# Other PSUM banks and slots for the first query blocks, and the exact squares of 26 chunk slots on ScalarE

## The chip, the cores and the metric

The kernel runs on one core of one Trainium2 chip. The core has five engines with queues of their own: TensorE (PE in the profile, its weight loads PEld), VectorE (DVE), ScalarE (ACT), GpSimd (POOL) and SyncE (SP), which here only issues DMAs. Each engine takes its instructions strictly in the order in which the program lists them, and waits where the next one waits. The metric is the device time of one execution in microseconds, the median of several executions.

## The reference

Three stages follow each other. All arithmetic is 32-bit.

```
attention: 4 batches, 8 heads, 576 positions, head size 64, each position sees itself and the 63 before it
  scores = q k^T / 8, masked; attn = exp(scores - max) / (sum + 1e-9); x = attn v        -> x: 2304 x 512
dense:     h = max(x w_in, 0)          w_in 512 x 2048
           x2 = (h * h) w_out          w_out 2048 x 512                                 -> x2: 2304 x 512
experts:   logits = x2 w_gate (8 experts); the largest logit chooses one expert per token
           out[token] = p(expert) * (max(x2 w1[e], 0) w2[e])     w1 512 x 1024, w2 1024 x 512
```

## The kernel before, in words

**Stages.** Tokens go through attention and the dense layer in 9 stages `st` of 256 tokens. A stage has four query blocks `g` of 64 positions, so blocks 0 to 7 belong to stages 0 and 1. The dense layer of a stage is 16 chunks `f` of 128 of the 2048 hidden units. One pair (st, f) is a chunk slot. `order` lists them: five slots of stage 0, then stages 0 and 1 in turn up to slot 26, the rest of stage 1 up to slot 31, then stage after stage. The experts follow from about 500 us on.

**Three matmuls for one.** An fp32 value is split into a rounded part `h` and a remainder `l`, and `mm3` (L172 to L174) multiplies h by h, h by l and l by h. Someone has to make these pairs: for x (`halves`, L168 on ACT and L169 on DVE), for the weights, and for the squared hidden units.

**One chunk slot.** `gemm1` makes 12 matmuls into one of two PSUM banks tagged `h`, in its first 256 columns. `hidden` (L462, ACT) writes r = relu. One slot later `square` (L469, ACT) writes gh = r squared, rounded, into SBUF, and DVE (L471) writes the exact square into columns 256 to 511 of the same bank; `square_low` (L478, DVE) subtracts: gl = exact minus gh. Two slots later `gemm2` makes 6 matmuls with gh and gl into the banks `y`. The bank `h` of a slot is free for the slot after the next when L478 has read it.

**Weights of the dense layer.** They arrive as 64-bit numbers that are rebuilt as fp32, per chunk f: two DMAs of 512 KB into one of two staging buffers `stg` (L236, L234), `conv_a` on ACT (L189), `conv_b` of four DVE instructions over 1024 columns (L205, L206, L207, L210), which at its end issues the loads of chunk f+2 into the same staging buffer, and `conv_c`: two casts on ACT (L226) and two subtractions on POOL or DVE (L228). Chunks are rebuilt while slots 0 to 26 run: one per slot for the first five slots, one per two slots after that. The same `tmp` buffers, two, hold what is being rebuilt.

**One query block.** `ATT` is a chain of steps, put at slot numbers by `chain`: scores on PE (L355 adds the mask for blocks below 8, L360), maximum on DVE (L375 and L378, or L383 and L387), four exps on ACT with their row sums `tot` (L396 for blocks below 8, L403 after that), `att_norm` (L410 and L411 on DVE: tot plus 1e-9, reciprocal; L412 on POOL: the product), four transposes on PE (L418), a copy on ACT (L423), 16 matmuls with v (L433), and the split of x (L168, L169). Scores of blocks 0 to 7 lie in the banks `y` 0 and 1 in turn, so block g+2 needs the exps of block g to be over.

**Order.** Slot i runs from -8 on; slots below 0 hold attention and weight rebuilding alone. What stands at one slot is emitted there in a fixed order, and a list scheduler then orders the instructions of each engine; the order is fixed in the program.

Of the kernel before, what the change touches and what calls it, by code (L numbers as in the profile page):

```python
# [16 lines left out]
ACTF = mybir.ActivationFunctionType  # L17
ALU = mybir.AluOpType
# [31 lines left out]
def kernel(  # L50
# [13 lines left out]
    nc = tc.nc  # L64
# [6 lines left out]
    NF = DFF // P  # L71
    ST = 256
    NS = NT // ST
    TT = ST // P
    QB = ST // W
# [47 lines left out]
    for half in range(2):  # L123
# [5 lines left out]
            out=mid, in_=mid, pattern=[[-1, P]], compare_op=ALU.is_ge, fill=NEG, base=W, channel_multiplier=1  # L129
# [25 lines left out]
    def psum(tag, bufs):  # L155
        return pr.tile([P, 512], F32, tag, bufs)

    ybanks = [pspool.tile([P, 512], F32, tag=f"y{i}", name=f"y{i}") for i in range(2 * TT)]
# [24 lines left out]
    def conv_a(f):  # L183
        i = (br.at["tmp"] + 1) % 4
        assert i % 2 == 0
        c = [br.tile([P, 512], I32, "tmp", 4) for _ in range(2)]
        whole = tmp2[i // 2].rearrange("p t n -> p (t n)")
        w = stg2[f % 2].bitcast(I32).rearrange("p t (n two) -> p (t n) two", two=2)
        nc.scalar.activation(whole.bitcast(F32), w[:, :, 1].bitcast(F32), ACTF.Abs)  # L189
        conv[f] = w[:, :, 0], w[:, :, 1], whole, c  # L190
# [109 lines left out]
    def load_q(g, n=1):  # L300
        b, i = divmod(g, NB)
        if g >= NE:
            qd[g] = br.tile([P, W, HP], F32, "qd", 1)
            nc.sync.dma_start(qd[g], qT[b, :, i])
            return
        qt = qfirst[:, g:g + n]
        for j in range(n):
            qk[g + j] = qfirst[:, g + j]
        if g > 1:
            for part in (qt[:D, :, W:], qt[D:, :, :W]):  # L310
                nc.scalar.copy(part, zero[:part.shape[0]].unsqueeze(2).unsqueeze(3).to_broadcast(part.shape))
        else:
            with tc.issue_after(made.ins):
                nc.vector.memset(qt[:D, :, W:], 0.0)
                nc.vector.memset(qt[D:, :, :W], 0.0)
        for half in range(2):
            rows = slice(half * D, half * D + D)
            nc.sync.dma_start(qt[rows, :, half * W:half * W + W, :], qT[b, rows, i:i + n])

    def lay_q(g):  # L320

        qk[g] = er.tile([P, HP, 2, W], F32, "q", 2)
        if g < NE + 2:
            with tc.issue_after(made.ins):
                nc.gpsimd.memset(qk[g][:D, :, 1, :], 0.0)
                nc.gpsimd.memset(qk[g][D:, :, 0, :], 0.0)
        d = qd.pop(g).rearrange("p s h -> p h s")
        for half in range(2):
            rows = slice(half * D, half * D + D)

            if g < NE + 5:
                nc.scalar.copy(qk[g][rows, :, half, :], d[rows])
            else:
                nc.gpsimd.tensor_copy(qk[g][rows, :, half, :], d[rows])  # L334
# [4 lines left out]
    def load_k(g, n=1):  # L339
        b, i = divmod(g, NB)  # L340
        nc.sync.dma_start(kfirst[:, g:g + n] if g < NB else kring[:, g % 4:g % 4 + n], kT[b, :, i:i + n])
# [7 lines left out]
    def att_scores(g):  # L349
        qt = qk.pop(g)  # L350
        k0 = g - 1 if g % NB else g
        if g < NE:
            ps = ybanks[g % 2]
            m = mask_b[:, 0 if g % NB else 1, :].unsqueeze(1).to_broadcast([P, HP, P])
            nc.tensor.matmul(ps.rearrange("p (h k) -> p h k", h=HP), lhsT=ident_b, rhs=m, start=True, stop=False)  # L355
        else:
            ps = psum("a", 2)
        for hp in range(HP):
            kt = kfirst[:, k0:k0 + 2] if g < NB else kring[:, k0 % 4:k0 % 4 + 2] if k0 % 4 < 3 else kring[:, 3::-3]
            nc.tensor.matmul(  # L360
                ps[:, hp * P:(hp + 1) * P], lhsT=qt[:, :, hp] if g < NE else qt[:, hp], rhs=kt[:, :, hp, :], start=g >= NE, stop=g >= NE or hp == HP - 1
            )
        if NE <= g < NS * QB - 1:
            lay_q(g + 1)
        if NE <= g < NS * QB - 2:
            load_q(g + 2)
        if NB < g < NS * QB - 3:
            load_k(g + 3)
        probs[g] = ps
# [20 lines left out]
    def att_exp(g):  # L390
        s, nmax = probs[g]
        tot = br.tile([P, HP], F32, "tot", 3)
        if g < NE:
            ps, s = s, sfirst[g % 4]
            for hp in range(HP):
                nc.scalar.activation(  # L396
                    s[:, hp, :], ps[:, hp * P:(hp + 1) * P], ACTF.Exp, bias=nmax[:, hp:hp + 1], scale=SCALE,
                    accum_out=tot[:, hp:hp + 1],
                )
            probs[g] = s, tot  # L400
            return
        for hp in range(HP):
            nc.scalar.activation(  # L403
                s[:, hp, :], s[:, hp, :], ACTF.Exp, bias=nmax[:, hp:hp + 1], accum_out=tot[:, hp:hp + 1]
            )
        probs[g] = s, tot

    def att_norm(g):
        s, tot = probs[g]
        nc.vector.tensor_scalar_add(tot, tot, 1.0e-9)  # L410
        nc.vector.reciprocal(tot, tot)  # L411
        nc.gpsimd.tensor_tensor(s, s, tot.unsqueeze(2).to_broadcast([P, HP, P]), op=ALU.mult)  # L412

# [51 lines left out]
    def square(st, f):  # L465
        ps, r = gT[st, f]
        gh = br.tile([P, ST], F32R, "gh", 3)
        gl = br.tile([P, ST], F32R, "gl", 3)
        nc.scalar.square(gh, r)  # L469

        nc.vector.scalar_tensor_tensor(  # L471
            out=ps[:, ST:2 * ST], in0=ps[:, :ST], scalar=0.0, in1=r, op0=ALU.max, op1=ALU.mult
        )
        gT[st, f] = ps, gh, gl

    def square_low(st, f):
# [403 lines left out]
    slot = {c: i for i, c in enumerate(order)}  # L880
    todo = {}
    ON_PE = (att_scores, att_transpose, att_values, gate_rank, early_pick, early_rows, early_tokens)

    def at(i, f, *args):
        todo.setdefault((i, f in ON_PE), []).append((f, args))

    def run(i, pe):
        for f, args in todo.pop((i, pe), ()):
            f(*args)
# [3 lines left out]
    def chain(i, stages, x, gaps, most=2):  # L893

        for f, gap in zip(stages, gaps):
            i += gap
            if f in ON_PE and i >= 0:
                while load.get(i, 0) >= most:
                    i += 1
                load[i] = load.get(i, 0) + 1  # L900
            at(i, f, x)
        return i

    ATT = (att_scores, att_max, att_exp, att_norm, att_transpose, att_evac, att_values, att_out)
    at(16, load_gates, 0)

# [2 lines left out]
            at(i + part, gate_dots, st, part)  # L909
        chain(i + E // 2, (gate_top, gate_rank, gate_slot), st, (0, 1, 1))  # L910

    PRE = 8
    for f in range(NF):
        i = max(-3, min(f - 1, slot[0, f] - 2))
        at(i, conv_c, f)
# [5 lines left out]
                  (0, load_k, 11), (0, load_k, 12), (0, load_wg, 0), (1, lay_q, NE), (1, load_q, NE + 1)):  # L921
        at(i, *l)
    for g in range(2 * QB):
        chain(g - PRE, ATT, g, (0, 1, 0, 1, 0, 1, 0, 1))
    for g in range(2 * QB, NS * QB):
        st, j = divmod(g, QB)
        i = slot[st, 0] - 19 + 4 * j
# [17 lines left out]
    conv_a(0)  # L945
    for i in range(-PRE, len(order) + LA):
        run(i, False)
        if 0 <= i - 1 < len(order):
            square(*order[i - 1])
            square_low(*order[i - 1])  # L950
        if 0 <= i < len(order):
            gemm1(*order[i])
        if i >= LA:
            st, f = order[i - LA]
            gemm2(st, f)
            if f == NF - 1:
                x2_out(st)
        run(i, True)
        if 0 <= i < len(order):
            hidden(*order[i])  # L960
# [194 lines left out]
```

## Time and profile before

| what | value |
| --- | --- |
| median of 3 runs | 835.53 us (834.1 to 836.63) |
| profiled execution, its own time | 832.06 us |
| span of its trace | 829.9 us |
| mean granted TensorE clock | 0.987 |
| busy: PE, PEld | 95%, 83% of the span |
| busy: DVE, ACT, POOL | 64%, 48%, 33% |

The span runs from the first to the last instruction; 2.16 us of the profiled execution lie around it. Busy shares are over the whole span and mix stages. The span has three stretches: the opening, in which attention of the first blocks and the weights of the dense layer are prepared; the dense stages from about 130 us; the experts from about 500 us. A matmul's row overlaps the next one's, so a row's own time is longer than the step from one to the next; the same holds, by a few hundredths of a microsecond, for DVE and ACT.

### The profile page before, as it was taken

How to read it: one execution, taken by the hardware profiler on the slowest of the kernel's cores; microseconds unless marked ns; L12 is line 12 of the kernel's file. 1: busy time of each engine (PE TensorE's matmuls, PEld its weight loads, DVE VectorE, ACT ScalarE, POOL GpSimd, SP SyncE). 2: the span in 40 equal slices, each digit the busy share in tenths (PEclk: the TensorE clock that was granted, in tenths of full speed). 3: DMA queues.
4: the chain of work that ended last, by engine and by line, in shares of the span. 5: the costliest groups of instructions: out<-in, count | busy, mean ns of one | idle time of the engine just before them, and what ended most of it. 6: DMA issues, size and time to landing. Idle time of an engine off the chain costs nothing.

```text
span 829.9 us, 14957 instructions
## 1 busy us (share of the span) xinstructions
PE 787.3 (95%) x5212; PEld 685.5 (83%) x5212; DVE 530.4 (64%) x1198; ACT 398.8 (48%) x1051; POOL 269.9 (33%) x262
## 2 busy tenths in 40 slices
PE   6889989999999999999999999989999999999894
PEld 5777878888888888888888897877898888888783
DVE  5799995984855947639467396568678654434110
ACT  6986663434444443534344345447577553434211
POOL 4646751112121221312211016165567541420201
PEclk9989999999999999999999999999999999999998
DMA  9845553111111111102020037366678644420101
GB/s 264 274 134 190 194 172 102 64 34 32 58 45 64 39 42 62 52 29 75 26 64 18 22 102 229 104 216 208 193 244 246 212 155 131 135 80 2 51 2 43
DMA packets 50860, 91.50 MB, mean 110 GB/s; under 512 B 8220, under 2 KB 24604, under 8 KB 50752
## 3 DMA queue, kind: packets, MB, share of 16 engines
q1 hardware_dynamic: 44688, 80.43, 30.3%
q0 software_dynamic: 6064, 9.63, 3.5%
q8 instruction: 69, 1.13, 0.6%
q14 instruction: 39, 0.32, 0.1%
HBM read 84.59 MB, written 13.81 MB: 119 GB/s over the span
## 4 chain that ended last, share of the span: by engine, by line
PE 66%; issue 13%; DVE 9%; DMA 5%; ACT 4%; POOL 1%; ACTq 0%; SPq 0%; POOLq 0%; DVEq 0%
PE h L172 11%; PE h L173 10%; PE h L174 10%; PE y L172 10%; PE y L174 9%; PE y L173 9%; PE a L360 2%; DMA stg<-in_moe_w_out 2%; PE a L433 2%; PE a L418 1%; DVE tmp L205 1%; DVE tmp L210 1%; PE a L683 1%; DVE tmp L207 1%; DMA out<-s,tab 1%
## 5 line engine op out<-in xcount | busy, mean ns | idle before, releaser
L172 PE MATMUL h<-xh,w 128*128 128x256 f32 (+3 forms) x864 | 262.9, 304 | 10.9 <-DVE gl L478 5.4
L174 PE MATMUL h<-xh,w 128*128 128x256 f32 (+3 forms) x864 | 255.6, 296 | 1.2 <-POOL w L228 1.2
L173 PE MATMUL h<-xl,w 128*128 128x256 f32 (+3 forms) x864 | 255.6, 296 | 0.9 <-DVE xl L169 0.5
L172 PEld LDWEIGHTS h<-xh,w 128*128 128x128 f32 x864 | 164.9, 191 | 27.6 <-DVE gl L478 9.6
L173 PEld LDWEIGHTS h<-xl,w 128*128 128x128 f32 x864 | 165.0, 191 | 9.1 <-DVE xl L169 0.9
L174 PEld LDWEIGHTS h<-xh,w 128*128 128x128 f32 x864 | 165.0, 191 | 4.3 <-POOL w L228 1.5
L462 ACT ACTIVATE r<-h 128x256 f32<-128x256 f32 x144 | 55.1, 382 | 203.7 <-PE h L174 197.9
L172 PE MATMUL y<-w,gh 128*128 128x512 f32 x294 | 119.2, 405 | 0.7 <-ACT gh L469 0.7
L770 DVE SCALAR_TENSOR_TENSOR ggl<-h,ggh 128x512 fp32r<-128x512 f32 (+1 forms) x69 | 46.2, 670 | 111.6 <-ACT ggh L769 111.5
L173 PE MATMUL y<-w,gh 128*128 128x512 f32 x294 | 116.4, 396 | 0.0
L471 DVE SCALAR_TENSOR_TENSOR h<-h,r 128x256 f32<-128x256 f32 x144 | 61.4, 426 | 84.0 <-ACT r L462 84.0
L174 PE MATMUL y<-w,gl 128*128 128x512 f32 x294 | 102.1, 395 | 0.5 <-DVE gl L770 0.5
L769 ACT ACTIVATE ggh<-h 128x512 fp32r<-128x512 f32 (+1 forms) x69 | 40.2, 583 | 125.5 <-PE h L174 96.2
L548 DVE SCALAR_TENSOR_TENSOR tmp<-tmp,stg 128x512 f32<-128x512 f32 x128 | 96.0, 750 | 0.8
L334 POOL COPY q<-qd 64x256 f32<-64x256 f32 x46 | 34.4, 749 | 143.9 <-PE a L360 142.5
L172 PE MATMUL y<-w,ggh 128*128 128x512 f32 x170 | 70.7, 416 | 0.0
L174 PE MATMUL y<-w,ggl 128*128 128x512 f32 x170 | 67.6, 398 | 1.7 <-DVE junk L996 1.1
L173 PE MATMUL y<-w,ggh 128*128 128x512 f32 x170 | 67.1, 395 | 0.0
L276 POOL TENSOR_TENSOR w<-stg,w 128x512 fp32r<-128x512 f32 x27 | 36.5, 1357 | 90.6 <-ACT w L275 87.6
L478 DVE TENSOR_TENSOR gl<-h,gh 128x256 fp32r<-128x256 f32 x144 | 60.5, 420 | 8.3 <-ACT gh L469 1.5
L172 PEld LDWEIGHTS y<-w,gh 128*128 128x128 f32 x294 | 55.6, 189 | 10.8 <-ACT gh L469 1.4
L173 PEld LDWEIGHTS y<-w,gh 128*128 128x128 f32 x294 | 55.6, 189 | 9.4
(165 smaller groups left out, 1262.4 us busy)
## 6 DMA issues: line engine op xcount, KB each, us to landing
stg<-in_moe_w SPq DMA_DIRECT2D x45, 512.0 KB, 4.0
stgx<-in_moe_w SPq DMA_DIRECT2D x18, 512.0 KB, 4.2
stg<-in_moe_w_in SPq DMA_DIRECT2D x16, 512.0 KB, 4.0
stg<-in_moe_w_out SPq DMA_DIRECT2D x16, 512.0 KB, 4.9
v<-in_v SPq DMA_DIRECT2D x28, 256.0 KB, 2.7
x_d<-tmp SPq DMA_DIRECT2D x18, 256.0 KB, 2.0
q<-in_moe_w SPq DMA_DIRECT2D x9, 512.0 KB, 4.5
qd<-in_q SPq DMA_DIRECT2D x28, 128.0 KB, 2.1
```

What stands on the lines that cost most here:

```text
L172: nc.tensor.matmul(o, lhsT=ah, rhs=bh, start=first, stop=False)
L173: nc.tensor.matmul(o, lhsT=ah, rhs=bl, start=False, stop=False)
L174: nc.tensor.matmul(o, lhsT=al, rhs=bh, start=False, stop=last)
L276: rest.tensor_tensor(l[:, a:a + 512], src, h[:, a:a + 512].bitcast(F32), op=ALU.subtract)
L334: nc.gpsimd.tensor_copy(qk[g][rows, :, half, :], d[rows])
L360: nc.tensor.matmul(ps[:, hp * P:(hp + 1) * P], lhsT=qt[:, :, hp] if g < NE else qt[:, hp], rhs=kt[:, :, hp, :], start=g >= NE, stop=g >= N ...
L462: nc.scalar.activation(r, gT[st, f][:, :ST], ACTF.Relu)
L471: nc.vector.scalar_tensor_tensor(out=ps[:, ST:2 * ST], in0=ps[:, :ST], scalar=0.0, in1=r, op0=ALU.max, op1=ALU.mult)
L478: nc.vector.tensor_tensor(gl, ps[:, ST:2 * ST], gh.bitcast(F32), op=ALU.subtract)
L548: nc.vector.scalar_tensor_tensor(out=junk, in0=x2sb[tt], scalar=1.0, in1=w, op0=ALU.mult, op1=ALU.mult, accum_out=l[:, t, e:e + 1])
L769: nc.scalar.activation(h[:, :width], hid[f][:, :width], ACTF.Relu)
L770: nc.vector.scalar_tensor_tensor(out=l[:, :width], in0=hid[f][:, :width], scalar=0.0, in1=h[:, :width].bitcast(F32), op0=ALU.max, op1=ALU. ...
```

## The change

Three edits, and what the scheduler makes of them.

- **Banks and slots of the first blocks.** Blocks 2 and 3 get their scores in the two banks `h`, which no slot uses yet; blocks 0 and 1 keep `y` 0 and 1, and 4 to 7 go on in those in turn. The first slot number goes from -8 to -6. Blocks 0 and 1 start at -6, 2 and 3 at -5, 4 and 5 at -3 (before: -8, -7, -6, -5, -4, -3), 6 and 7 at -2 and -1 as before.
- **The 1e-9 on ACT.** For all 36 blocks it is added by an ACT instruction behind the exps instead of a DVE instruction before the reciprocal.
- **The exact squares of slots 0 to 25.** There ACT writes r squared into columns 256 to 511 of the bank `h`, and a second ACT instruction copies it, rounded, from there into gh. DVE's L471 is gone in these slots. From slot 26 on nothing changes here.

```
 def att_scores(g):
-            ps = ybanks[g % 2]
+            ps = psum("h", 2) if g in (2, 3) else ybanks[g % 2]
 def att_exp(g):                      # once in each of the two branches
+            nc.scalar.activation(tot, tot, ACTF.Copy, bias=1.0e-9)
 def att_norm(g):
-        nc.vector.tensor_scalar_add(tot, tot, 1.0e-9)
         nc.vector.reciprocal(tot, tot)
 def square(st, f):
-        nc.scalar.square(gh, r)
-        nc.vector.scalar_tensor_tensor(
-            out=ps[:, ST:2 * ST], in0=ps[:, :ST], scalar=0.0, in1=r, op0=ALU.max, op1=ALU.mult
-        )
+        if slot[st, f] < 2 * NF - 6:
+            nc.scalar.square(ps[:, ST:2 * ST], r)
+            nc.scalar.copy(gh, ps[:, ST:2 * ST])
+        else:
+            nc.scalar.square(gh, r)
+            nc.vector.scalar_tensor_tensor(
+                out=ps[:, ST:2 * ST], in0=ps[:, :ST], scalar=0.0, in1=r, op0=ALU.max, op1=ALU.mult
+            )
...
-    PRE = 8
+    PRE = 6
...
     for g in range(2 * QB):
-        chain(g - PRE, ATT, g, (0, 1, 0, 1, 0, 1, 0, 1))
+        chain(g // 2 - PRE if g < QB else max(-3, g - 2 * QB), ATT, g, (0, 1, 0, 1, 0, 1, 0, 1))
```

The line numbers of the new kernel are higher by one to eight: L396 is L397, L423 is L425, L462 is L464, L478 is L485; the new instructions are L401, L408, L474 and L475.

On ACT, in the start of the program, the kernel before has this (nmax and sf are the maxima and the exps of one block; sf_143 is block 3, tmp_76 and tmp_77 the weights of chunks 0 and 1).

```order
L396 ACTIVATE sf_140,tot_183<-y_131,nmax_178 128x128 x4
L378 ACTIVATE nmax_179<-nmax_179 128x4
L396 ACTIVATE sf_141,tot_184<-y_132,nmax_179 128x128 x4
L378 ACTIVATE nmax_180<-nmax_180 128x4
L396 ACTIVATE sf_142,tot_185<-y_131,nmax_180 128x128 x4
L189 ACTIVATE tmp_77<-stg_79 128x1024
L226 CAST w_271<-tmp_76 128x4x128
L226 CAST w_272<-tmp_76 128x512
L378 ACTIVATE nmax_178<-nmax_178 128x4
L423 COPY sf_140<-a_204 128x512
L423 COPY sf_141<-a_205 128x512
L396 ACTIVATE sf_143,tot_183<-y_132,nmax_178 128x128 x4
```

And now, in the same place:

```order
L397 ACTIVATE sf_140,tot_188<-y_131,nmax_183 128x128 x4
L379 ACTIVATE nmax_184<-nmax_184 128x4
L401 ACTIVATE tot_188<-tot_188 128x4
L397 ACTIVATE sf_141,tot_189<-y_132,nmax_184 128x128 x4
L379 ACTIVATE nmax_185<-nmax_185 128x4
L401 ACTIVATE tot_189<-tot_189 128x4
L397 ACTIVATE sf_142,tot_190<-h_203,nmax_185 128x128 x4
L379 ACTIVATE nmax_183<-nmax_183 128x4
L401 ACTIVATE tot_190<-tot_190 128x4
L189 ACTIVATE tmp_77<-stg_79 128x1024
L397 ACTIVATE sf_143,tot_188<-h_204,nmax_183 128x128 x4
```

The exps of block 3 stand ahead of the two casts of chunk 0 and the two copies of blocks 0 and 1, which followed block 2 before; blocks 2 and 3 are read from the banks h.

On ACT in the middle of the opening, around slots 8 to 10, before:

```order
L462 ACTIVATE r_461<-h_435 128x256
L469 ACTIVATE gh_81<-r_461 128x256
L462 ACTIVATE r_460<-h_434 128x256
L226 CAST w_271<-tmp_77 128x4x128
L226 CAST w_272<-tmp_77 128x512
L469 ACTIVATE gh_82<-r_460 128x256
```

And now:

```order
L464 ACTIVATE r_456<-h_204 128x256
L408 ACTIVATE tot_188<-tot_188 128x4
L332 COPY q<-qd_405 64x4x64 x2
L474 ACTIVATE h_204<-r_456 128x256
L168 CAST xh<-a_233 128x4x64
L189 ACTIVATE tmp_77<-stg_79 128x1024
L475 CAST gh_82<-h_204 128x256
L226 CAST w_243<-tmp_76 128x4x128
L226 CAST w_244<-tmp_76 128x512
```

Between relu and gh there is now one more instruction of the slot, and others can stand on either side of it.

On DVE in the same stretch, before (L205 to L210 are the weights, L471 and L478 a chunk slot):

```order
L207 SCALAR_TENSOR_TENSOR tmp_76<-stg_78,tmp_76 128x1024
L387 TENSOR_REDUCE nmax_180<-s_1063 128x4
L478 TENSOR_TENSOR gl_85<-h_434,gh_82 128x256
L210 SCALAR_TENSOR_TENSOR tmp_76<-stg_78,tmp_76 128x1024
L471 SCALAR_TENSOR_TENSOR h_435<-h_435,r_461 128x256
L478 TENSOR_TENSOR gl_83<-h_435,gh_80 128x256
L410 TENSOR_SCALAR tot_185<-tot_185 128x4
L411 RECIPROCAL tot_185<-tot_185 128x4
L205 TENSOR_SCALAR tmp_77<-tmp_77 128x1024
```

And now:

```order
L207 SCALAR_TENSOR_TENSOR tmp_77<-stg_79,tmp_77 128x1024
L485 TENSOR_TENSOR gl_83<-h_203,gh_80 128x256
L169 TENSOR_TENSOR xl<-y_133,xh 128x4x64
L210 SCALAR_TENSOR_TENSOR tmp_77<-stg_79,tmp_77 128x1024
L485 TENSOR_TENSOR gl_84<-h_204,gh_81 128x256
L205 TENSOR_SCALAR tmp_76<-tmp_76 128x1024
```

The square and the addition are gone from between the weights; the subtraction stays. The order of the DMAs on SP changes by a few places only.

## Rows read from the trace of the kernel before

**Rows 1.** The page: busy tenths of three engines in 40 slices of 20.75 us.

```profile
PE   6889989999999999999999999989999999999894
DVE  5799995984855947639467396568678654434110
ACT  6986663434444443534344345447577553434211
```

**Rows 2.** Windows: stretch, its length, busy us (count) per engine, clock, DMA share, GB/s.

```profile
10.00:70.00 60.00, 50.64 (x402) 43.70 (x402) 52.47 (x87) 52.19 (x162) 33.01 (x23) 0.94 0.70 226
34.00:70.00 36.00, 31.44 (x244) 26.47 (x245) 33.95 (x55) 31.18 (x82) 19.99 (x13) 0.91 0.48 158
54.50:61.50 7.00, 5.75 (x23) 5.13 (x24) 6.83 (x13) 6.96 (x25) 4.08 (x3) 0.51 0.34 116
70.00:130.00 60.00, 55.09 (x382) 46.62 (x381) 59.58 (x87) 36.20 (x87) 32.77 (x23) 1.00 0.54 181
130.00:480.00 350.00, 350.00 (x2578) 310.47 (x2577) 226.96 (x698) 146.38 (x475) 66.96 (x78) 1.00 0.15 46
```

**Rows 3.** Waits of PE from 70 to 130 us: us in total, times, longest.

```profile
PE h L172 <- DVE gl L478: 3.4, 6, 1.1
```

**Rows 4.** Timeline of the start: start us, us, engine, line, operation, idle before and releaser.

```profile
10.91 0.20 ACT L378 ACTIVATE nmax<-nmax 128x4 f32<-128x4 f32 x1
12.52 0.21 ACT L378 ACTIVATE nmax<-nmax 128x4 f32<-128x4 f32 x1
12.70 0.58 PE L355 MATMUL y<-mask_b,ident_b 128*128 128x512 bf16 x1 [3.25 <-ACT sf L396]
15.87 0.21 ACT L378 ACTIVATE nmax<-nmax 128x4 f32<-128x4 f32 x1 [1.59 <-DVE nmax L375]
...
17.49 1.13 ACT L189 ACTIVATE tmp<-stg 128x1024 f32<-128x1024 f32 x1
...
21.97 0.24 ACT L378 ACTIVATE nmax<-nmax 128x4 f32<-128x4 f32 x1
...
34.28 0.50 PE L172 MATMUL h<-xh,w 128*128 128x256 f32 x2 [1.11 <-ACT xh L168]
```

**Rows 5.** Groups by line, 70 to 130 us: count, busy us, mean ns, idle before.

```profile
L210 DVE SCALAR_TENSOR_TENSOR tmp<-stg,tmp 128x1024 int32<-128x1024 int32 x9 | 11.4, 1263 | 0.0
...
L471 DVE SCALAR_TENSOR_TENSOR h<-h,r 128x256 f32<-128x256 f32 x17 | 7.1, 419 | 0.0
L478 DVE TENSOR_TENSOR gl<-h,gh 128x256 fp32r<-128x256 f32 x16 | 6.6, 410 | 0.1
...
L410 DVE TENSOR_SCALAR tot<-tot 128x4 f32<-128x4 f32 x3 | 0.5, 157 | 0.0
...
L469 ACT ACTIVATE gh<-r 128x256 fp32r<-128x256 f32 x16 | 6.7, 417 | 0.4
L462 ACT ACTIVATE r<-h 128x256 f32<-128x256 f32 x17 | 6.4, 376 | 8.3 <-PE h L174 8.3
```

**Rows 6.** Timeline of DVE, 116 to 125 us: one chunk of weights and its neighbours.

```profile
116.68 1.21 DVE L210 SCALAR_TENSOR_TENSOR tmp<-stg,tmp 128x1024 int32<-128x1024 int32 x1
...
118.15 0.68 DVE L205 TENSOR_SCALAR tmp<-tmp 128x1024 f32<-128x1024 f32 x1
...
122.68 0.42 DVE L471 SCALAR_TENSOR_TENSOR h<-h,r 128x256 f32<-128x256 f32 x1
123.01 1.21 DVE L210 SCALAR_TENSOR_TENSOR tmp<-stg,tmp 128x1024 int32<-128x1024 int32 x1
...
124.48 0.68 DVE L205 TENSOR_SCALAR tmp<-tmp 128x1024 f32<-128x1024 f32 x1
```

**Rows 7.** Timelines of SP and ACT, 117 to 125 us: the staging buffer's next load.

```profile
117.96 0.38 SPq L236 DMA_DIRECT2D stg<-in_moe_w_in  x1
118.44 0.44 SPq L234 DMA_DIRECT2D stg<-in_moe_w_out  x1
...
123.21 1.20 ACT L189 ACTIVATE tmp<-stg 128x1024 f32<-128x1024 f32 x1 [2.38 <-DMA stg<-in_moe_w_out]
```

More of the change, by code (lines that the diff above doesn't have):

```diff
@@ L405, in att_exp @@
             )
+        nc.scalar.activation(tot, tot, ACTF.Copy, bias=1.0e-9)
         probs[g] = s, tot
```

## The prediction

> **What bounds the kernel now.** I read the slices of the page first [rows 1]. PE is at 9 tenths nearly everywhere; its holes before the experts lie in the first six slices, and there DVE is at 9 tenths from the third to the sixth. So I asked for windows [rows 2]. From 130 to 480 us PE is busy 350 of 350 us: nothing that the change does to DVE or ACT there can shorten anything, and what the opening gains or loses is passed on as it is. From 70 to 130 us DVE is busy 59.58 of 60 us and PE 55.09: DVE is the bound, PE idles 4.91 us. The waits of PE in that stretch say how the bound reaches it [rows 3]: six times, 3.4 us in all, the first matmul of a slot waits for L478, the subtraction that frees its bank h. From 10 to 70 us no engine is full for long: PE idles 9.4 us, DVE 7.5, ACT 7.8, and 4.56 us of PE's are behind 34 us. From 54.5 to 61.5 us, after waits of PE, the granted clock is 0.51, so nearly all of it at the lower level of 1.2 GHz: half of 7 us, some 3.4 us, is lost there.
>
> So the change can act in two places: the start, up to the first matmul of slot 0 at 34.28 us [rows 4], and the stretch to about 130 us.
>
> **The start.** Slot 0 needs blocks 0 to 3. Before, the mask of block 2 waits 3.25 us until ACT has read block 0's bank; ACT then waits 1.59 us for block 2's maximum [rows 4], and block 3's exps stand behind L189, two casts and two copies, ending at 21.97 us, where the next L378 starts. Now blocks 2 and 3 need no bank of another block. ACT's step from one block to the next is 12.52 - 10.91 = 1.61 us. Four of them, three additions of 0.21 us (the nearest row is L378 over the same 4 elements) and L189 with 1.13 us give 10.91 + 6.44 + 0.63 + 1.13 = 19.1 us for the end of block 3's exps, 2.9 us sooner. That rests on queries and keys of blocks 2 and 3 having landed by about 12.5 us; block 2's mask at 12.70 was held by ACT and its scores followed with no DMA wait. Bounds: 0, if something behind (the reciprocal behind chunk 1's weights on DVE, POOL, a landing) keeps slot 0 where it is, and 4.8 us, both waits in full. I take 3.0, since the row of ACT's step is the chain's own.
>
> Is it kept to 70 us? ACT is the engine that could take it back. By 70 us it gains 8 additions, 1.7 us, and a second instruction for seven slots, 0.42 us each, 2.9 us. Its idle time is 7.8 us [rows 2], so 3.2 us of room remain: enough for the 3.0, and for nothing more. I therefore count the other holes of PE between 34 and 70 us, and the low clock, as unchanged.
>
> **The squares.** Slots 0 to 25 lose L471 on DVE. Its row is 419 ns long [rows 5], but instructions overlap: L471 at 122.68 is followed by L210 at 123.01 [rows 6], so a square costs DVE 0.33 us. From 70 to 130 us there are 17 of them and three L410 of 0.157 us or less: 17 x 0.33 + 3 x 0.1 = 5.9 us off DVE's 59.6. Before 70 us the same saving (6 squares) lies beside an ACT that has no room, and the three after 130 us beside a full PE; both count as nothing. If that cover were gone they would be worth 9 x 0.33 = 3 us more.
>
> ACT pays: gh took one instruction (L469, 417 ns), now a square and a copy. The trace shows no ACT write from SBUF into PSUM. The nearest rows are L469 with 417 ns (SBUF to SBUF) and L462 with 376 ns (PSUM to SBUF); the price is bounded by nothing, if only the copy matters for the chain, and by 2 x 417 ns in series. I take 0.42 us per slot, by L469: 17 x 0.42 = 7.1 us more in a stretch in which ACT is busy 36.2 of 60 us. 43.3 of about 53 us is still no bound.
>
> The Trainium skill speaks against this move: "ScalarE: Activation LUTs", section "Rules for kernel authors", says to do relu, max and products on VectorE, which it gives as up to three times as fast per element in bf16. The trace does not bear that out for these fp32 tiles: L471 on DVE 419 ns, L469 on ACT 417 ns over the same 128x256 [rows 5]. By the rule ACT's part would be dear, which is the slower rival below; by the rows the two engines cost the same and only their load decides.
>
> What is late next, once DVE has room? Two things. PE itself: it idles 4.91 us there, so no more can come of it. And the staging loop: L210 at 116.68 ends at 117.89, the next load is issued at 117.96 and 118.44, L189 starts on its landing at 123.21 after a wait of 2.38 us, and L205 starts at 124.48 [rows 6, 7]. That is 6.6 us from the end of one chunk's L210 to the L205 of the chunk after the next, in which DVE had no time over. With c for DVE's time from L205 to L210 of a chunk, two chunks can't take less than 6.6 + c. Before, c is 123.01 + 1.21 - 118.15 = 6.1 us [rows 6], so the floor is 6.35 us per chunk; without two squares c is 5.4 and the floor 6.0. DVE alone would need 6.7 - 0.7 = 6.0 us, 6.7 being 60 us over the nine L210 of the stretch [rows 5]. The loop thus costs little, but it is close. Of the cap of 4.91 us I take 4.0; bounds 0 and 4.9.
>
> **The 1e-9.** On DVE it is counted. On ACT it stands behind the exps, 0.21 us later for the reciprocal; past 130 us it lies beside 350 us of full PE, with ACT busy 146 of them. Nothing, at most 36 x 0.21 us if every block stood on the path, which rows 2 exclude.
>
> **The sum.** 3.0 + 4.0 = 7.0 us off the profiled execution: 832.06 - 7.0 = 825.1 us, span 822.9 us plus 2.16 around it. The median of the runs shown is 3.5 us above that execution, and the metric is such a median: 835.5 - 7.0 = 828.5 us.
>
> **The rivals.** *Little of it.* By 70 us ACT takes the start back: the additions and copies also stand in front of the casts of the weights, which PE waits for. After 70 us the staging loop, a little longer than in rows 7, holds the chunks at their old pace. For it: L189 already waits for its DMA 2.38 us, and ACT is nearly full from 54.5 to 61.5 us, 6.96 of 7 [rows 2]. Against it: DVE's work truly shrinks by a tenth where it is the bound. It would leave 0.5 of the start and 1.0 of the rest: 834.0 us.
>
> *All of it.* The start brings 3.0, PE's idle 4.9 us after 70 us go, the low clock from 54.5 us does not come because PE no longer waits ahead of it (3.4), and 2 of the 4.56 us go too: 13.3 us, 822 us. For it: each of these is idle time of PE that hangs on DVE or ACT. Against it: ACT's room of 3.2 us, and the weights of the first five slots, which come no sooner than their DMAs.
>
> *Slower: the chain of gl through ACT.* Before, the exact square on DVE and gh on ACT ran beside each other; now relu, square, copy and subtraction follow each other, and on ACT other work (L189, casts of 1.1 us a pair, q copies) stands between square and copy. PE waits for just this, through the bank h [rows 3]. Each slot loses 0.33 us of DVE's queue ahead of gl and gains at least 0.42 us on ACT; it decides from the point where what stands between the two ACT instructions exceeds what DVE lost, some 0.3 us per slot on average. With 0.42 us more at each of 17 slots PE waits 7.1 us longer, less the 3.0 of the start: 4.1 us slower, 839.6 us. For it: six of these waits are there now. Against it: gl and the bank are each wanted only two slots after the slot's own gemm1, and DVE's queue ahead of L478 shrinks.
>
> That the change doesn't do what it says is not a rival: the rows of the instructions show both moves.
>
> **How the numbers follow.** The forecast 0.48, all of it 0.18, little of it 0.16, slower 0.18. The likeliest one's own range follows from its bounds (start 0 to 4.8, squares 0 to 4.9): both upper ends give 825.8 us, and with one lower end and the other term as taken it is 831.5 or 832.5, so 826 to 832.5 us. To hold 8 in 10 the range must take in most of "all" and "little" and the near part of "slower": 821 to 838 us. A measurement of this kernel can tell about 0.3%, 2.5 us, from no change. "Little" at 1.5 us lies within that, with a quarter of it beyond on the faster side: faster 0.48 + 0.18 + 0.04 = 0.70, same 0.12, slower 0.18.
>
> **What would show it.** In the profile after, the first matmul of slot 0 starts near 31 us instead of 34.28; if it starts at 34, the start failed. The exps of block 3 end near 19 us. From 70 to 120 us DVE is below 59.6 of 60, ACT above 43 of 60 in proportion, and L478's line as what PE waits for shrinks from 3.4 us; if it grows, the slower rival is right. L189's waits for the staging DMAs grow a little; if they grow to a microsecond per chunk and DVE idles before L205, the loop holds. The dense stages are full on PE and start some 7 us sooner. The prediction is wrong if they start at the same time or later, or over 12 us sooner.

## The result, and the profile after

The changed kernel takes 839.3 us (median of 17 runs, 835.48 to 841.76) against 834.1 us (17 runs, 831.67 to 837.11). The ratio is 1.0056, interval 1.0042 to 1.0071: 4.7 us slower, where 7.0 us faster was forecast. Its profiled execution has a span of 837.1 us (before 829.9).

Two rows of the page answer to [rows 1]:

```profile
PE   6789889999999999999999999979999999999894
DVE  5699993894764946639467387567677654434110
```

The tenths hardly move: PE's row is a tenth lower in three slices, and DVE is still at 9 from the third to the sixth. So the windows, in the columns of [rows 2], of the kernel after:

```profile
34.00:70.00 36.00, 29.25 (x236) 24.85 (x237) 34.40 (x47) 31.99 (x90) 17.86 (x12) 0.95 0.47 156
54.50:61.50 7.00, 6.68 (x46) 5.63 (x45) 6.96 (x9) 5.44 (x11) 3.12 (x3) 1.00 0.49 165
70.00:130.00 60.00, 52.40 (x372) 43.26 (x372) 58.87 (x66) 41.11 (x106) 35.61 (x25) 1.00 0.56 183
130.00:480.00 350.00, 350.00 (x2579) 310.59 (x2578) 218.55 (x670) 149.91 (x501) 67.27 (x78) 1.00 0.15 46
```

PE idles 6.75 us instead of 4.56 from 34 to 70 us and 7.60 instead of 4.91 from 70 to 130: 4.9 us more. That is about the size of the loss, but no exact account of it: by the granted clock from 34 to 70 us, 0.95 instead of 0.91, some 1.4 us of it came back (an estimate from these rows), and PE has not done the same steps by 34 us. From 130 us on PE is full as before; the last relu of the dense stages starts at 526.25 us instead of 521.41, 4.8 us later. The other 2.4 us between the two spans lie in the experts; what follows the last relu takes 308.5 us before, and 308.5 to 314.3 in the traces of the kernels of the table below. DVE has 21 instructions less from 70 to 130 us and is busy 0.7 us less.

The start, in the columns of [rows 4], the last exp of block 3 and the first two matmuls of slot 0:

```profile
18.68 0.37 ACT L397 ACTIVATE sf<-h,nmax 128x128 f32<-128x128 f32 x1
...
32.94 0.48 PE L172 MATMUL h<-xh,w 128*128 128x256 f32 x2
```

The exps of block 3 end at 19.05 us, as worked out (19.1). Slot 0 begins 1.3 us sooner, not 3.0. Groups of the kernel after, 70 to 130 us (columns of [rows 5]):

```profile
L207 DVE SCALAR_TENSOR_TENSOR tmp<-stg,tmp 128x1024 int32<-128x1024 int32 x9 | 17.0, 1891 | 0.2
L206 DVE TENSOR_SCALAR tmp<-tmp 128x1024 int32<-128x1024 int32 x9 | 12.5, 1388 | 0.1
...
L485 DVE TENSOR_TENSOR gl<-h,gh 128x256 fp32r<-128x256 f32 x15 | 6.1, 409 | 0.0
L474 ACT ACTIVATE h<-r 128x256 f32<-128x256 f32 x15 | 5.8, 387 | 0.3
L475 ACT CAST gh<-h 128x256 fp32r<-128x256 f32 x15 | 5.5, 370 | 0.2
```

The same two weight instructions in the kernel before, same stretch:

```profile
L207 DVE SCALAR_TENSOR_TENSOR tmp<-stg,tmp 128x1024 int32<-128x1024 int32 x9 | 13.8, 1530 | 0.0
...
L206 DVE TENSOR_SCALAR tmp<-tmp 128x1024 int32<-128x1024 int32 x9 | 10.2, 1137 | 0.0
```

Nothing was done to L206 and L207, yet nine of each take 5.5 us more. The squares that left took 17 x 0.33 = 5.6 us; that the two numbers nearly match is no rule, since with the order held the same squares gone lengthen the weights by 1.7 us of 7.9 (the table over 13 chunks further down).

Which waits hold PE from 34 to 130 us (us in total, times, longest)? After:

```profile
PE h L172 <- DVE gl L485: 4.3, 5, 1.7
PE a L361 <- ACT sf L425: 2.2, 1, 2.2
PE y L172 <- ACT gh L475: 1.8, 2, 1.1
PE a L435 <- DVE s L384: 1.6, 1, 1.6
PE a L361 <- DVE xl L169: 1.5, 1, 1.5
PE a L420 <- POOL s L414: 1.4, 1, 1.4
PE h L173 <- DVE xl L169: 1.0, 1, 1.0
PE a L420 <- POOL sf L414: 0.9, 1, 0.9
PE a L361 <- DVE s L384: 0.3, 1, 0.3
```

And before:

```profile
PE h L172 <- DVE gl L478: 3.7, 7, 1.1
PE a L418 <- DVE s L383: 1.5, 1, 1.5
PE h L174 <- POOL w L228: 1.2, 1, 1.2
PE h L172 <- ACT w L226: 1.1, 1, 1.1
PE h L172 <- ACT xh L168: 1.1, 1, 1.1
PE h L173 <- DVE xl L169: 0.5, 1, 0.5
PE a L360 <- DVE s L383: 0.5, 1, 0.5
PE y L172 <- ACT gh L469: 0.5, 1, 0.5
```

Read them in two heaps. The waits of chunk slots (`h` and `y`) are 8.1 us before and 7.1 after. The waits of attention steps (`a`: scores, transposes, values of a block) are 2.0 before and 7.9 after. PE takes its row strictly in order, so an attention step whose input isn't ready stops the chunk slots behind it. One such place, PE and ACT of the kernel after, 41 to 47 us:

```profile
43.30 1.16 PE L361 MATMUL a<-kf,q 128*128 128x128 f32 x8 [2.17 <-ACT sf L425]
...
46.18 0.36 PE L172 MATMUL h<-xh,w 128*128 128x256 f32 x1
```

```profile
41.05 1.31 ACT L332 COPY q<-qd 64x256 f32<-64x256 f32 x2
42.39 0.37 ACT L168 CAST xh<-y 128x256 fp32r<-128x256 f32 x1
42.66 0.59 ACT L425 COPY sf<-a 128x512 f32<-128x512 f32 x1
43.13 0.39 ACT L475 CAST gh<-h 128x256 fp32r<-128x256 f32 x1
```

The scores of block 8 stand in PE's row ahead of slot 2 and wait 2.17 us for the copy that empties their bank, which stands on ACT behind two q copies; a gh (L475) stands there too. Slot 2's first matmul starts at 46.18 us. Before, it starts at 42.16, and the scores of block 8 come behind it, at 46.39.

This place shows the mechanism, not the lag that stays. Attention steps that now stand ahead of slot 2 stood behind it before, and the next slots are level again: slot 3's relu starts at 54.76 us against 54.73, slot 6's at 68.53 against 69.06. The lag that stays comes behind 70 us. Slot 12's relu starts 2.4 us later (93.63 against 91.23), slot 24's 5.1; before, and after:

```profile
132.76 0.38 ACT L462 ACTIVATE r<-h 128x256 f32<-128x256 f32 x1 [0.63 <-PE h L174]
```

```profile
137.86 0.39 ACT L464 ACTIVATE r<-h 128x256 f32<-128x256 f32 x1 [1.59 <-PE h L174]
```

PE's waits from 70 to 130 us alone, after:

```profile
PE h L172 <- DVE gl L485: 3.8, 4, 1.7
PE a L435 <- DVE s L384: 1.6, 1, 1.6
PE a L361 <- DVE xl L169: 1.5, 1, 1.5
PE y L172 <- ACT gh L475: 0.7, 1, 0.7
```

Before, they were 3.4 us for gl [rows 3] and the 1.5 us of L418 above. So attention steps make 1.6 us of the 2.7 us more, the slots' gh and gl the rest. PE also does the transposes and values of one block more there (16 and 64 matmuls against 12 and 48), some 1.3 us by its rows (0.66 us for four transposes, 0.69 for 16 matmuls with v). What makes up the rest of this lag isn't shown.

### The profile page after: what moved, and what is told of

The parts are those of the page before. It is cut to its first block, busy times and chain, and to the rows that moved or that the text cites. A ratio compares the mean times of both kernels' runs of the same rounds, so it can differ in the third digit from the quotient of the medians.

```text
span 837.1 us, 14934 instructions
## 1 busy us (share of the span) xinstructions
PE 788.3 (94%) x5212; PEld 685.8 (82%) x5212; DVE 519.4 (62%) x1136; ACT 409.9 (49%) x1113; POOL 270.6 (32%) x262
## 5 line engine op out<-in xcount | busy, mean ns | idle before, releaser
L464 ACT ACTIVATE r<-h 128x256 f32<-128x256 f32 x144 | 55.2, 384 | 192.9 <-PE h L174 190.5
L478 DVE SCALAR_TENSOR_TENSOR h<-h,r 128x256 f32<-128x256 f32 x118 | 50.7, 429 | 79.4 <-ACT r L464 79.2
L555 DVE SCALAR_TENSOR_TENSOR tmp<-tmp,stg 128x512 f32<-128x512 f32 x128 | 94.1, 735 | 0.8
L485 DVE TENSOR_TENSOR gl<-h,gh 128x256 fp32r<-128x256 f32 x144 | 60.4, 420 | 32.0 <-ACT gh L477 15.2
L414 POOL TENSOR_TENSOR s<-s,tot 128x512 f32<-128x512 f32 x28 | 32.5, 1162 | 102.9 <-DVE tot L413 86.0
L172 PEld LDWEIGHTS y<-w,gh 128*128 128x128 f32 x294 | 55.6, 189 | 12.4 <-ACT gh L475 2.8
```

The source lines that it names most:

```text
L172: nc.tensor.matmul(o, lhsT=ah, rhs=bh, start=first, stop=False)
L464: nc.scalar.activation(r, gT[st, f][:, :ST], ACTF.Relu)
L478: nc.vector.scalar_tensor_tensor(out=ps[:, ST:2 * ST], in0=ps[:, :ST], scalar=0.0, in1=r, op0=ALU.max, op1=ALU.mult)
L485: nc.vector.tensor_tensor(gl, ps[:, ST:2 * ST], gh.bitcast(F32), op=ALU.subtract)
L555: nc.vector.scalar_tensor_tensor(out=junk, in0=x2sb[tt], scalar=1.0, in1=w, op0=ALU.mult, op1=ALU.mult, accum_out=l[:, t, e:e + 1])
```

## The experiments

All are medians over five rounds beside the kernel before on the same chip; two further runs, named below, are one execution each. Theory A: what DVE saves comes back as longer instructions beside POOL. B: the chain of gl through ACT. C: the order that the scheduler makes. D: the staging loop.

| run | median, us | ratio to before, interval | PE idle 34 to 160 us |
| --- | --- | --- | --- |
| before | 834.1 | | 9.5 |
| the changed kernel | 839.3 | 1.0056, 1.0042 to 1.0071 | 14.4 |
| squares alone | 835.9 | 1.0016, 1.0003 to 1.0029 | 11.2 |
| banks alone | 843.21 | 1.0104, 1.0076 to 1.0133 | 14.6 |
| 1e-9 alone | 839.84 | 1.0075, 1.0055 to 1.0095 | 14.8 |
| changed, L228 on DVE | 832.72 | 0.9982, 0.9966 to 0.9999 | 8.6 |
| 1e-9, old order | 833.8 | 0.9996, 0.998 to 1.0013 | 9.5 |
| squares, old order | 833.04 | 0.9988, 0.9974 to 1.0002 | 9.9 |
| banks, old order | 834.87 | 1.0011, 0.9996 to 1.0025 | 9.8 |
| all three, old order | 834.41 | 1.0005, 0.9989 to 1.0022 | 9.3 |
| before, L228 on DVE | 837.97 | 1.0041, 1.0024 to 1.0058 | 15.0 |
| all three in that order | 840.41 | 1.0079, 1.0054 to 1.0104 | 15.3 |
| squares twice, old order | 840.3 | 1.0066, 1.0043 to 1.009 | 15.6 |
| before in the order of "1e-9 alone" | 843.65 | 1.0107, 1.0082 to 1.0133 | 17.9 |
| all three, only DVE's row old | 837.41 | 1.0038, 1.0022 to 1.0055 | 11.8 |
| changed, L228 on DVE, two ACT rules | 834.04 | 1.0003, 0.999 to 1.0015 | 9.9 |
| squares, L228 on DVE | 832.54 | 0.9976, 0.996 to 0.9992 | 8.6 |
| squares, 1e-9, L228 on DVE | 836.79 | 1.0023, 1.0006 to 1.0041 | 11.7 |

The last column (126 us less PE's busy time in the window 34 to 160 us) is of the one profiled execution. It goes with the time, though not in proportion: wherever a kernel is 3 us or more slower, PE idles 2 us or more longer there. The windows behind four of its values, in the columns of [rows 2]; before:

```profile
34.00:160.00 126.00, 116.53 (x817) 100.11 (x818) 113.54 (x195) 79.39 (x202) 57.92 (x40) 0.97 0.44 146
```

the changed kernel:

```profile
34.00:160.00 126.00, 111.65 (x802) 95.32 (x803) 106.97 (x148) 86.89 (x234) 58.63 (x41) 0.99 0.45 146
```

all three edits in the old order:

```profile
34.00:160.00 126.00, 116.73 (x819) 100.85 (x820) 107.64 (x161) 89.95 (x239) 57.76 (x40) 0.97 0.45 148
```

and the kernel before in the order of "1e-9 alone":

```profile
34.00:160.00 126.00, 108.13 (x771) 91.89 (x772) 109.51 (x170) 76.50 (x201) 56.39 (x40) 0.97 0.45 148
```

The third has DVE 5.9 us less busy than the first, and PE as busy: DVE's relief did not reach PE. Of PE's waits from 34 to 160 us in the third, those for gl are down from 3.7 us and those for gh, now behind a square and a copy on ACT, up from 0.5; its waits for xh and xl, for weights from ACT and POOL and for s stay, 5.3 us of them against 5.9:

```profile
PE y L172 <- ACT gh L473: 2.6, 3, 2.1
PE h L172 <- DVE gl L483: 1.9, 4, 1.0
```

In the fourth DVE and PE are both less busy than in the first: PE waits for gl and gh (further down), and DVE is idle 16.5 us instead of 12.5.

**One edit at a time.** The first edit alone is `psum("h", 2) if g in (2, 3)` with PRE and chain, the second the 36 additions, the third the `if slot[st, f] < 2 * NF - 6` of `square`. The fourth run is the changed kernel with

```
-            low = nc.vector if (2 * f + which) % 6 == 5 else nc.gpsimd
+            low = nc.vector
```

> The kernel before with the third edit alone: the exact squares of slots 0 to 25 on ScalarE; the banks, the slots of the first blocks and the 1e-9 stay as they were. Theory A (VectorE and GpSimd get in each other's way on SBUF: after the change L206 and L207 each took 0.24 and 0.32 us longer beside GpSimd's L228, and that ate what the squares gave): VectorE stays full from 70 to 130 us, L206 and L207 are again longer than before (above 1.25 and 1.65 us on average), the rebuilding of the weights is no sooner, and the time is within 1.5 us of the kernel before. Theory B (the chain relu, square, copy, subtraction through ScalarE): this edit carries the loss, 3 to 6 us slower than before, and PE waits for gl several us longer than 3.7. My forecast's own reading, that the squares bring 4.0 us, would give 830.

> The kernel before with the first edit alone: blocks 2 and 3 in the banks h, first slot -6 and the new slots of blocks 0 to 5. Theory A, with the second half of it (the order written out for VectorE and PE puts attention and weights further ahead of the chunk slots): slot 0 begins about 1 us sooner, slots 2 to 16 then fall behind, and the edit alone costs 2 to 4 us. Theory B: slot 0 begins 1 us sooner and that is kept, 0.5 to 1.5 us faster. My forecast's reading was 3 us faster.

> The kernel before with the second edit alone: the 1e-9 added on ScalarE for all 36 blocks. Both theories: nothing that can be told, within 1 us of the kernel before. If it is more, the additions stand in ScalarE's queue in front of something that PE waits for.

> The changed kernel with all 32 subtractions of the weights (L228) on VectorE, where one in six was; GpSimd keeps the products of the blocks. From 34 to 130 us that is 21 more for VectorE. Theory A: alone they take 0.68 us each (the nearest row is L384, 677 ns over the same 128x512), 14 us in all, and L206 and L207 fall from 1.35 and 1.83 us to about 0.7 and 1.2 us, which gives 14 x (0.67 + 0.62) = 18 us back: the weights are ready some 4 us sooner and the time is 1 to 6 us below that of the changed kernel. Without such a hindrance (theory B): VectorE, full from 34 to 130 us, gets 21 x 0.99 us = 21 us more by the row of L228 on it, and the kernel is 10 to 20 us slower than the changed one.

Alone the edits cost 1.3, 8.7 and 6.3 us by their ratios, 16 in all; together 4.7. Such a sum is no sum of costs. Theory B loses ground: its edit costs least. The 36 additions, 0.2 us each, cost 6.3 us, and only some 14 of them run while PE isn't full. But of DVE's first 230 instructions, which reach to about 158 us, nearly half (104) stand outside the longest sequence that the old row and the new one share (the expectation further down counts places, not sequence). That points to theory C, which the next runs test. Moving L228 brought 6.2 us against the changed kernel, at the upper end of what theory A had. Groups of that run, 70 to 130 us:

```profile
L228 DVE TENSOR_TENSOR w<-tmp,w 128x512 fp32r<-128x512 f32 x19 | 14.5, 789 | 1.0 <-ACT w L226 1.0
L207 DVE SCALAR_TENSOR_TENSOR tmp<-stg,tmp 128x1024 int32<-128x1024 int32 x9 | 11.1, 1235 | 0.0
...
L206 DVE TENSOR_SCALAR tmp<-tmp 128x1024 int32<-128x1024 int32 x9 | 6.5, 726 | 0.1
```

With GpSimd's subtractions gone L206 falls from 1.39 to 0.73 us and L207 from 1.89 to 1.24.

**The same edits in the old order.** Edges without waits hold the row of every engine to that of the kernel before, in short:

```
+    for p, q in zip(row, row[1:]):     # row: the engine's instructions as they stood before
+        tc.add_manual_dep(q, p.name, DependencyInfo(NoSync, DATA), reason="order")
```

> The 1e-9 on ScalarE alone, as in e1_tot, but every engine's order in the opening and the dense stages is held to that of the kernel before (order edges, no waits; the 36 additions leave VectorE's row and stand on ScalarE right behind the four exps of their block). e1_tot was 5.4 us slower, with VectorE's rows standing otherwise in two thirds of their places. Theory C (the loss is the new order that the scheduler made, not the edits): within 1 us of the kernel before. If the additions themselves cost it, 4 to 6 us slower again.

> The exact squares of slots 0 to 25 on ScalarE alone, in the order of the kernel before (the 26 L471 are gone from VectorE's row; on ScalarE the copy to gh stands right behind the square). Theory A (what VectorE saves comes back as longer L206 and L207 beside GpSimd): within 1 us of the kernel before, and from 70 to 130 us L206 and L207 are longer than 1.14 and 1.53 us. Theory C with my forecast's size for the squares: 2 to 4 us faster. Theory B (the chain of gl through ScalarE): 2 to 5 us slower, with PE's waits for gl grown from 3.4 us.

> Blocks 2 and 3 in the banks h, nothing else, in the order of the kernel before. e1_banks was 8.8 us slower with its new order. Theory C: 0 to 1.5 us faster, since block 2's mask no longer waits 3.25 us, while block 3's exps still stand behind L189 and the casts. If the banks h themselves cost it (slot 0 must wait until ScalarE has read them), 2 to 9 us slower.

> Banks, 1e-9 and squares together, in the order of the kernel before. Theory C: the sum of the three runs beside it, 2 to 6 us faster than before where the changed kernel is 4.7 us slower. Theory A alone: 0 to 1.5 us faster. If it is 4 us slower again, the order is not the cause.

All four stand within 1.0 us of before by their ratios, and each interval holds 1. The banks that cost 8.7 us, and the additions that cost 6.3, cost nothing that can be told here. Of the first edit only the banks are left here: the new slots of the first blocks are nothing but order. So the edits do not carry the loss: of the 4.7 us of the changed kernel 0.4 are left in the old order. (The kernel before, held to its own order, was not run; that the edges themselves cost nothing rests on these four.) Theory C's gain of 2 to 6 us did not come either: the squares bring 1.0 us (interval 2.2 faster to 0.2 slower), as theory A had it.

**What holds the saving back.**

> The kernel before with all 32 subtractions of the weights (L228) on VectorE, in the order that the scheduler then makes. VectorE gets 21 more from 34 to 130 us, 0.79 us each by the row of e1_low_on_dve, 16.6 us, and by theory A loses 13.5 x (0.43 + 0.30) = 10 us of lengthened L206 and L207: some 6 us more work for a full engine, 2 to 6 us slower than before. Without theory A it loses nothing and is 10 us slower or more.

> The kernel of e3_before_low_on_dve with the banks, the 1e-9 and the squares changed and every engine's order held to that of e3_before_low_on_dve. Theory A: with GpSimd's subtractions gone nothing of what the squares save can come back as longer L206 and L207, so the same edits that brought 0 in the order of the kernel before (e2) bring 3 to 5 us here, against e3_before_low_on_dve. Theory D (the loop over the staging buffer holds the chunks, whatever VectorE does): again nothing, within 1 us of e3_before_low_on_dve.

> The kernel before, its order held, with the exact square (L471) of slots 0 to 25 made twice in a row on VectorE: 17 more of 0.33 us from 70 to 130 us, 5.7 us, 26 x 0.33 = 8.6 us in all. If VectorE is the bound there, 4 to 7 us slower. Theory A lets a part be absorbed, since squares read PSUM and shorten L206 and L207 by standing beside GpSimd's work: 2 to 5 us slower. Theory D (the staging loop is the bound): less than 1.5 us slower.

> All three edits in the order of the kernel before (as e2_all_in_old_order), with the loads of chunks 2 to 15 cut to half their columns; the other half of a staging buffer keeps what the chunk before left there, so the weights and the routing are others, and only the opening and the dense stages are compared. Theory D: L189's waits for the DMA go, the L210 of chunk 15 starts 2 to 4 us sooner than the 128.99 us of e2_all_in_old_order and the last relu of the dense stages as much sooner than 522.0. Theory A: less than 1 us on either.

The first is 3.4 us slower, as A had it. The second falls against A in its strict form: with L228 on DVE the edits gave no 3 to 5 us but lost 3. DVE is 7.8 us less busy there from 34 to 160 us (102.43 against 110.24) and PE is no busier: it waits 10.8 us for gh (8.7 without the edits), in an order whose row wasn't made for them. L206 and L207 take as long in both (25.2 and 25.1 us over 13 chunks), so there it is not they that hold the saving back. The squares made twice (`square`'s DVE instruction repeated) cost 5.5 us of the 8.6 added: DVE's load does count, upwards, as a full DVE has it (4 to 7) and a little more than A had (2 to 5). The half loads (one execution; `wst[n][:, :512]` and half of each w_in block) meet both marks of D: L210 of chunk 15 starts at 126.55 us instead of 128.99, and the last relu at 519.59 instead of 522.02. But 1.44 us of that are there at L210 of chunk 2, with slot 0 sooner by as much; over the 13 chunks the loads give 1.0 us. So D is a small part there, and not the bound.

**The order alone, and the rest of the saving.**

> The kernel before, no edit at all, with every engine's order held to the one that the scheduler made for e1_tot (the 36 additions back on VectorE, each right before its reciprocal; nothing else differs from e1_tot). Theory C (the order alone costs the time): 3 to 7 us slower than before, as e1_tot was 5.4. If the additions on ScalarE in that order did it (they stand in front of casts there): within 1.5 us of before.

> The kernel before, its order held, with the exact squares of slots 0 to 25 left out on both engines: ScalarE makes gh as before, and gl is taken against the unsquared columns, so the numbers and the routing are others and only the opening and the dense stages are compared. This is VectorE's saving without ScalarE's part. If the chain through ScalarE ate the saving in e2_squares_in_old_order (theory B): the 13 chunks from L210 of chunk 2 to that of chunk 15 take 89 us or less, where e2_squares_in_old_order took 93.6 and before 94.3, and the last relu of the dense stages comes 4 us or more ahead of 521.4. Theory A (it comes back as longer instructions beside GpSimd): 91.5 us or more, L206 and L207 together 2 us or more longer in that span than before, and the last relu less than 3 us ahead.

> Banks, 1e-9 and squares as in e2_all_in_old_order, but only VectorE's row is held to the order of the kernel before; the scheduler orders the other four engines. Theory C, if it is VectorE's row that counts (it is the full engine): 0 to 1.5 us from before, as e2_all_in_old_order was. If ScalarE's or TensorE's row counts as much: 2 us or more slower.

> e1_low_on_dve (the changed kernel with all L228 on VectorE, 832.7 us) in its own order, but for two rules on ScalarE: the 1e-9 of a block stands right behind its four exps (for block 9 it stood behind L189, a relu and two q copies, and VectorE waited 1.1 us for it), and the q copies (L332, 1.3 us a pair) go six places later, behind casts that PE waits 1.8 us for. Theory C: 1 to 3 us faster than e1_low_on_dve, 829.5 to 832, which would beat both kernels. If those waits are covered by VectorE's load anyway: within 1 us of e1_low_on_dve.

The first run settles that order alone can cost this much: the instructions of the kernel before, not one changed, in another order, are 8.9 us slower. (It is the order of "1e-9 alone"; the order of the changed kernel was not run without its edits.) In that order the edit costs nothing: "1e-9 alone" is 2.7 us faster than it by the ratios, though the intervals overlap. Its PE waits, 34 to 160 us, stand elsewhere than in the changed kernel:

```profile
PE h L172 <- DVE gl L478: 11.1, 10, 2.2
PE y L172 <- ACT gh L469: 3.8, 2, 3.3
PE a L418 <- POOL sf L412: 1.1, 1, 1.1
```

Here gl is late, there the attention steps. Holding DVE's row alone is not enough: 3.2 us slower, so the other rows count too. The two rules for ACT by hand made their base no faster (1.8 us slower by the ratios, where 1 to 3 faster was expected); waits that they took away came back as others (PE now waits 1.8 us for the q copies).

The run without squares (one execution: L471 left out, nothing added on ACT) weighs A against B. Sums of DVE from the L210 of chunk 2 to that of chunk 15, worked out from the timelines (an instruction counts until the next begins):

| us of DVE over 13 chunks | before | squares, old order | no squares, old order | changed |
| --- | --- | --- | --- | --- |
| exact squares | 7.9 | 0 | 0 | 0 |
| weights, L205 to L210 | 59.8 | 61.5 | 62.0 | 66.9 |
| L228 on DVE | 5.3 | 6.4 | 6.3 | 4.6 |
| reciprocals and additions | 1.7 | 2.7 | 2.8 | 0.7 |
| idle | 2.5 | 5.5 | 4.4 | 2.7 |
| the rest | 17.2 | 17.5 | 17.4 | 16.9 |
| span | 94.3 | 93.6 | 92.9 | 91.8 |

Each column is one execution; the runs of the banks and of the 1e-9 in the old order have a span of 94.5 us, 0.2 above before. With the squares gone and nothing in their place, 7.9 us leave and 1.4 come off the span. 4.4 went into the same weights, L228 and additions made longer, 1.9 into waits. The last relu starts at 521.67 us, no sooner than before (521.41), as slot 0 came 0.9 us later. With the squares on ACT the span is 0.7 us longer, and 3.0 us instead of 1.9 go into waits. So A over B, with waits as a second part. Of A's own mark, L206 and L207 together 2 us or more longer, 1.4 came (35.66 against 34.27 us at full length); what else of the 4.4 there is lies in L205, L210, L228 and the additions. In the changed kernel 7.1 us went into longer weights, yet its rebuilding is 2.5 us shorter and L210 of chunk 15 starts at 128.84 us against 129.42: it does not lose for late weights.

**Two more orders.**

> The squares of slots 0 to 25 on ScalarE and all L228 on VectorE, without the banks and the 1e-9, in the order that the scheduler makes of it. If moving L228 is what made e1_low_on_dve 6.6 us faster than the changed kernel (GpSimd out of VectorE's way), it does as well here, on e1_squares (835.9): 829 to 833. Theory C (the order that comes with each edit counts more): anywhere from 830 to 842, and as likely slower than e1_squares as faster.

> The same with the 1e-9 on ScalarE too, without the banks; again in the order that the scheduler makes of it. If moving L228 is what counts: 829 to 833. Theory C: 830 to 842, and more than 3 us from e5_squares_low_on_dve in either direction, though the edit between them was worth 0 in a held order.

They stand 3.9 us apart by the ratios, though the edit between them is worth nothing in a held order: C again. The first is 2.0 us faster than before and 6.7 faster than the changed kernel, the best of the study together with the changed kernel with L228 on DVE (1.5 faster than before), from which it can't be told. That moving L228 is what makes it so is not settled: of three kernels with and without the move two gained by it (the changed kernel, squares alone) and one lost (before).

## Why the prediction was wrong

- **Place: right; bound: half.** The dense stages end 4.8 us later and lost it in the opening; PE is full from 130 us. DVE is full from 70 to 130 us, and more work on it costs time (the squares twice). But work taken off it did not come off the time: in the old order DVE is 5.9 us less busy and PE busy as before.
- **The start, 3.0 us: mis-sized.** ACT did what was worked out (19.05 us against 19.1); slot 0 gained 1.3. The scores of blocks 4 to 7 still share two banks, and two maxima waited 2.55 and 2.46 us for scores from PE; whether the banks made them wait was not tested. The bank by itself, in the old order, is worth nothing that can be told.
- **"I therefore count the other holes of PE between 34 and 70 us, and the low clock, as unchanged": the step that failed.** I had looked only at ACT's room of 3.2 us, and shown the moved rows without pricing them; behind 70 us I priced the squares alone and took the order for given in the same way. In its place: PE's holes grew by 2.2 us from 34 to 70 us and, where 4.0 us were to go, by 2.7 from 70 to 130 us, with attention steps in PE's row ahead of their inputs (7.9 us of such waits against 2.0). The old order takes 4.3 of the 4.7 us away; another order costs 8.9 us with no edit. Which moved instruction costs what is read from one trace, not tested one by one. The low clock did go (54.5 to 61.5 us at 1.00 instead of 0.51), and 60 to 70 us is at 0.83 instead.
- **The squares, 4.0 us: mis-sized.** The instructions are as priced: ACT's square 387 ns and copy 370 against one of 417, so 0.34 us more (0.42 taken). The Trainium skill's rule against such work on ACT ("ScalarE: Activation LUTs", "Rules for kernel authors") gives its figure for bf16; for these fp32 tiles it is not borne out: the move costs nothing that can be told in the old order. But taking 5.6 us off a full DVE was held to make 5.6 us of room. In the old order PE's idle from 70 to 130 us fell from 4.91 to 3.81 with the squares, and even with the exact square on neither engine only 1.4 us came off 13 chunks. Weights, L228 and additions grew beside POOL, DVE stood idle for part of it, and only 3.4 us of PE's holes there had hung on gl at all. The rows that I had chosen, [rows 5, 6], show L205 and L210 and neither L206 nor L207.
- **The staging loop: right**, costs little (half the loads gave 1.0 us over 13 chunks). **The 1e-9 at nothing: right** in a held order.
- **The rivals.** The slower one, 839.6 us, meets the time and not the cause: PE's waits for gl from 70 to 130 us went from 3.4 to 3.8 us, not up by 7, and the same chain in the old order costs nothing that can be told. No rival had the order itself as its mechanism, though the rows showed it rewritten.

## What to carry to other kernels

Where a list scheduler sets the order, an edit of a few small instructions can rewrite every engine's row, and that alone was worth up to 9 us here: hold the order to price the edit, or price the order, by what stands in the bound engine's row ahead of the critical work and whether its input is ready there. Time taken off a full engine is room only if what fills it doesn't stretch, and only for the waits that hang on that engine: look at an instruction's length alone and beside its neighbours, and at who waits for it, before counting it. Edits measured one at a time in orders of their own don't add up.

## What the hardware showed that was not expected

In the kernel before, 20 to 135 us, DVE's L206 takes 0.67 to 0.69 us with POOL idle and up to 1.69 beside POOL's L228; the exact squares and gl, one operand in PSUM, take 0.39 to 0.43 us either way. Chunk 15 in both kernels, DVE and POOL; before:

```profile
125.41 1.69 DVE L206 TENSOR_SCALAR tmp<-tmp 128x1024 int32<-128x1024 int32 x1
```

```profile
125.26 1.29 POOL L228 TENSOR_TENSOR w<-tmp,w 128x512 fp32r<-128x512 f32 x1 [3.59 <-ACT w L226]
```

and after:

```profile
124.74 0.70 DVE L206 TENSOR_SCALAR tmp<-tmp 128x1024 int32<-128x1024 int32 x1
```

```profile
124.84 1.73 POOL L228 TENSOR_TENSOR w<-tmp,w 128x512 fp32r<-128x512 f32 x1 [3.29 <-ACT w L226]
```

Whoever starts second is longer: L206, begun 0.15 us after L228, ends 0.55 us after it, and L228, begun 0.10 us after L206, takes 0.44 us more. The Trainium skill, "SBUF — State Buffer", section "Terms", says that VectorE and GpSimd share a port pair that one instruction holds to its end while the other blocks; these rows agree.

ACT's write from SBUF into PSUM, of which before had no row, is no dearer than its others: L474 387 ns over 128x256, against 417 from SBUF to SBUF (L469) and 376 from PSUM to SBUF (L462).
